# Window attention and two feed-forward layers: weights decoded in pairs, scores and values handled for two groups at once, and one fixed order for three engines

## The chip, the core and the metric

The kernel runs on one core of a Trainium2 chip. The metric is the device time of one execution in microseconds (us); less is better. TensorE (PE in the rows, PEld its weight loads) does the matrix products, VectorE (DVE), ScalarE (ACT) and GpSimd (POOL) the elementwise work, and SyncE (SP) issues every DMA of this kernel.

## What is computed

```python
# q, k, v: (4, 8, 576, 64) float32; weights arrive as float64
scores = q @ k.T / sqrt(64);  window: 0 <= pos_q - pos_k < 64, else -1e9
attn = softmax(scores);  x = (attn @ v) -> (2304, 512)
x = maximum(maximum(x @ w1, x @ w2), x @ w3) @ w_out        # 512 -> 768 -> 512
h = x @ w_in                                               # 512 -> 2048
g = h where h >= 1, 0 where h <= -1, else (h + 1)**2 / 4
out = g @ w_out2                                           # 2048 -> 512, float32 (2304, 512)
```

## The kernel before

The 2304 tokens are 36 groups of 64 queries (9 for each batch entry). The first stage works on 9 blocks of 256 tokens (4 groups each), the second on blocks of 512.

**Weights.** Each float64 weight tile (128 rows by 512 columns) is loaded by one 512 KB DMA into a staging buffer `wst` (`w_load`, 4 buffers) and decoded by `w_split` into a high and a low float32 part: two ACT passes over the two 32-bit words (L165, then L108 with `wst` as output), a DVE shift (L169) and a DVE add (L170) into `wt`, an ACT copy for the high part (`u<-wt` or `v<-wt`) and a POOL subtraction for the low part (L111). 24 tiles belong to the first feed-forward layer (buffers `u`), 32 to the second (8 in buffers `v`, then the 24 `u` again). Every product is three matmul passes: high by high, high by low, low by high.

**Attention**, for a group: `load` and `vload` bring q, k, v; `prep` transposes q and k (on PE and out of PSUM for groups 0 to 15, on DVE after that); `qk` makes 8 score matmuls into `sps` (L288) and, right behind them, four DVE reductions with the mask (L293, result `sm` and the row minimum `nm`); `ex` is four ACT exponentials; `norm` a DVE reciprocal and a POOL product; `ptr` four PE transposes into `pps` and `ptc` their ACT copy; `pv` 8 matmuls into `ops` (L342), an ACT copy and a DVE subtraction into the token tile `xt`. `sps` and `ops` are one PSUM tile each with room for two groups.

**First feed-forward layer**, for a block: 18 `a_item`s (L363, 12 matmuls each, PSUM tile `ps` out of 3 buffers), three of which make one of six hidden tiles: ACT copies the first product (`ht`), DVE takes two maxima (L372), ACT and POOL split the result into `h`. Then four `b_item`s (L385, 18 matmuls), whose result ACT copies to `x2s` (2 buffers) and SP stores to `x_scratch`.

**Order.** Everything of the first stage gets a place on a time line in units of one `a_item`; `put` collects, a sort sets the order. From the third block on, groups are handled in pairs at *visits*, one each 12 units: at a visit PE does `pv` of one pair, `ptr` of the next, `qk` of the one after. The `b_item`s of a block come `BD` = 6 items into the next block. From the first visit on, each step's PE instructions are tied behind those of the step before (`chained`, `tc.issue_after`); the scheduler sets everything else, and the whole of the start. Shortly before the last block (`put(begin[...] - 0.1, None)`, the *turn* below) the attention's memory is given to the second layer, whose weights follow by `w2_next`.

**Second layer**: for each block and hidden tile, `c_mm` (L541, 12 matmuls), `c_act` (two ACT, three DVE instructions) and, three steps later, `d_item` (L606, 12 matmuls). `x2_split` loads (`x2r`) and splits the block's input.

Of the kernel before, what the change touches and what calls it, by code (L numbers as in the profile page):

```python
# [21 lines left out]
NW = 4  # L22
# [26 lines left out]
EXP = (1.1, 2.1)  # L49
PTC = (0.6, 1.6)  # L50

# [3 lines left out]
    "T2 X2 T3 X3 W6"  # L55
# [5 lines left out]
def kernel(ctx, tc, q, k, v, w1, w2, w3, wo1, wi2, wo2, out, x2d):  # L61
# [92 lines left out]
    def w_split(key, st, eng):

        s = wslot[key]
        hi, lo = st[:, :, 1], st[:, :, 0]
        t = stg.tile([P, 512], I32, tag="wt", name="wt", bufs=WT)
        nc.scalar.activation(  # L165
            hi.bitcast(F32), hi.bitcast(F32), AF.Prelu, scale=2.0 ** (WS - 119), alpha=2.0 ** 32
        )
        act_copy(lo, lo.bitcast(U32), scale=2.0 ** -29)
        nc.vector.tensor_scalar(t, hi, 3, None, op0=ALU.logical_shift_left)  # L169
        nc.vector.tensor_tensor(t, t, lo, op=ALU.add)  # L170
        act_copy(s[:, 0:512], t.bitcast(F32))
        sub(eng, s[:, 512:1024], t.bitcast(F32), f32(s[:, 0:512]))

    def w_col(key, hl, kt):
        return wslot[key][:, hl * 512 + kt * P: hl * 512 + (kt + 1) * P]
# [14 lines left out]
    def load(g):  # L190
# [15 lines left out]
        if g not in pet and (g - PET) % CH == 0:  # L206
            for nm, src in (("q", q), ("k", k)):
                t = stg.tile([P, NP, 2 * CH, 32], F32, tag="wst", name="raw", bufs=NW)
# [12 lines left out]
                chunk[nm, (g - PET) // CH] = t  # L221

    def vload(g):
        b, i, s = blk(g)
        s0 = i * BL
        d = st_g[g]
        if g == 0:
            return
        t = apool.tile([P, H, D], F32, tag="vr", name="vr", bufs=5)
# [45 lines left out]
    def qk(g):  # L275
        d = st_g[g]
        win, mask, W = window(g)
        sm = apool.tile([P, NP, 2 * BL], F32, tag="sm", name="sm", bufs=5)
# [3 lines left out]
        for x in range(2):  # L282
            for bank in range(2):
                p = 2 * bank + x
                for h in range(2):
# [4 lines left out]
                    )  # L290

        for p in range(NP):
# [4 lines left out]
        d.update(sm=sm, nm=nm, W=W)  # L297

    def ex(g):
        d = st_g[g]  # L300
        W, sm = d["W"], d["sm"]
        ss = apool.tile([P, NP], F32, tag="ss", name="ss", bufs=5)
        for p in range(NP):
# [3 lines left out]
        d["ss"] = ss  # L307
# [19 lines left out]
    def ptc(g):  # L327
# [3 lines left out]
        act_copy(pt[0:W], d["pps"][0:W])  # L331
        d["pt"] = pt

    def pv(g, xt, off):
# [10 lines left out]
        act_copy(xt[:, 0, :, off:off + BL], ops)  # L345
        sub(nc.vector, xt[:, 1, :, off:off + BL], ops, f32(xt[:, 0, :, off:off + BL]))
# [47 lines left out]

    def x2_split(tb, pool, kt):
        t0, n = blocks2[tb]
        if kt == 0:
            x2t[tb] = pool.tile([P, 2, KD, N2], F32R, tag="x2t", name="x2t", bufs=1)
        x = x2t[tb]
        r = pool.tile([P, N2], F32, tag="x2r", name="x2r", bufs=2)  # L400
        nc.sync.dma_start(r[:, 0:n], x2d[kt, :, t0:t0 + n])
        act_copy(x[:, 0, kt, 0:n], r[:, 0:n])
        sub(nc.vector, x[:, 1, kt, 0:n], r[:, 0:n], f32(x[:, 0, kt, 0:n]))
# [26 lines left out]
    def pv_x(g):  # L430
        j, o = gblock[g]
        if o == 0:
            xt_new(j)
        pv(g, xts[j], o)
# [37 lines left out]
    for cost, fn, args in seq:  # L472
# [3 lines left out]
        if args[0] == 0:  # L476
            put(at + 0.5, w_next, nc.gpsimd)
# [7 lines left out]
    stages = (load, vload, prep, qk, ex, norm, ptr_c, pv_x)  # L485
    ops0 = dict(L=load, V=vload, P=prep, Q=qk, E=ex, N=norm, T=ptr_c, X=pv_x)
    for x, tok in enumerate(SEQ.split()):
        if tok[0] == "W":
            for _ in range(int(tok[1:] or 1)):
                put(-100 + 0.1 * x, w_next, nc.gpsimd)  # L490
# [30 lines left out]
    put(begin[len(blocks1) - 1] - 0.1, None)  # L521

    order2 = [(w, f) for f in range(KF2) for w in (4, 5)]
    slots2, w2n = [], [0]

    def w2_next():
        n = w2n[0]
        if n < len(order2):
            w, f = order2[n]
            st = w_load((w, f), wi2 if w == 4 else wo2, slots2[n], "col" if w == 4 else "row", f)  # L530
            w_split((w, f), st, nc.gpsimd)
            w2n[0] += 1
# [14 lines left out]
    tail = [None]  # L547

    def chained(fn, *args):

        if tail[0] is None:
            fn(*args)
        else:
            with tc.issue_after(tail[0]):
                fn(*args)
        pe = [i for i in nc.cur_bb.bb.instructions[-200:] if i.engine == mybir.EngineType.PE]
        if pe:
            tail[0] = pe[-1]

    for at, _, fn, args in order:  # L560
        if fn:
            if (fn, args) == (b_item, (len(blocks1) - 1, 0)):
                c_mm(0, 0, pacc, "acc")
            if at < visits[0]:
                fn(*args)
            else:
                chained(fn, *args)
        else:
# [3 lines left out]
            slots2 += [p2.tile([P, 1024], F32R, name=f"v{i}") for i in range(2 * KF2 - NU)] + U  # L572
            for kt in range(KD):
                x2_split(0, p2, kt)
            for _ in range(4):
                w2_next()
# [42 lines left out]
    for x, (tb, f) in enumerate(seq):  # L619
# [39 lines left out]
```

## Time and profile before

| | |
|---|---|
| median of 3 runs | 863.98 us (861.62 to 864.16) |
| the profiled execution's own time | 864.39 us |
| its span, first to last instruction | 862.3 us |
| PE busy / DVE / ACT / POOL | 798.3 / 363.9 / 356.2 / 157.9 us |
| mean granted clock of TensorE | 0.985 of full |

The span is what a page of the profile divides up; 2.1 us of the execution's own time lie around it. Busy times are those of single engines and overlap each other. "Idle before" in a row is the time that the engine stood still just ahead of it, with the instruction that released it.

### The profile page before, as it was taken

The page shows a single profiled execution, that of the slowest core. Times are in us where ns is not written, and L with a number is a line of the kernel's source. Part 1 is how long each engine was busy: PE and PEld are TensorE (multiplying, and loading weights), DVE is VectorE, ACT ScalarE, POOL GpSimd, SP SyncE. Part 2 cuts the span into 40 slices and gives each one's busy share as a digit, 9 for nine tenths or more (in the row PEclk, how much of TensorE's full clock was granted, in tenths as well). Part 3 has the DMA queues.
Part 4 walks back from the last instruction along what each step waited for, and adds up shares of the span by engine and source line. Part 5 has one row for each costly group of instructions (what it writes and reads, how often), then busy time and mean ns, then how long its engine had stood idle before and what let it go on. Part 6 is the DMA issues. An engine that isn't in the chain of part 4 may idle for free.

```text
span 862.3 us, 14835 instructions
## 1 busy us (share of the span) xinstructions
PE 798.3 (93%) x5776; PEld 701.6 (81%) x5776; DVE 363.9 (42%) x937; ACT 356.2 (41%) x871; POOL 157.9 (18%) x157
## 2 busy tenths in 40 slices
PE   6698889999999898999779999999999999999998
PEld 4597778889898888898778888888888888888896
DVE  5778422323333432316678733433343334333343
ACT  6988533333333534324779422322232223222232
POOL 3666311111111121213574200000000000000000
PEclk8899999999999999999989999999999999999999
DMA  9976243233141413003777000100020001000000
GB/s 243 279 216 187 43 84 85 52 70 63 40 80 32 135 26 98 14 26 111 234 222 241 24 1 25 62 0 1 1 74 0 1 1 36 25 1 1 24 26 25
DMA packets 128054, 62.70 MB, mean 73 GB/s; under 512 B 98288, under 2 KB 120816, under 8 KB 127984
## 3 DMA queue, kind: packets, MB, share of 16 engines
q1 hardware_dynamic: 127984, 61.76, 26.2%
q8 instruction: 45, 0.74, 0.4%
q14 instruction: 25, 0.20, 0.1%
HBM read 52.30 MB, written 9.44 MB: 72 GB/s over the span
## 4 chain that ended last, share of the span: by engine, by line
PE 77%; DVE 5%; DMA 4%; ACT 4%; issue 2%; SPq 1%; POOL 1%; DVEq 0%; ACTq 0%; POOLq 0%
PE acc L606 23%; PE hp L541 23%; PE ps L363 18%; PE ps L385 7%; DMA wst<-in_moe_w_in 3%; PE ops L342 2%; PE sps L288 2%; PE pps L324 1%; DVE sm L293 1%; SPq L215 1%; DVE wt L170 1%; DMA x2r<-x_scratch 1%; ACT wst L165 1%; DVE wt L169 1%; ACT wst L108 1%
## 5 line engine op out<-in xcount | busy, mean ns | idle before, releaser
L363 PE MATMUL ps<-xt,u 128*128 128x256 f32 x1944 | 239.1, 283 | 9.1 <-DVE ht L372 4.0
L363 PEld LDWEIGHTS ps<-xt,u 128*128 128x128 f32 x1944 | 232.5, 190 | 13.9 <-DVE ht L372 5.2
L541 PE MATMUL hp<-x2t,u 128*128 128x512 f32 (+1 forms) x720 | 161.6, 372 | 0.0
L606 PE MATMUL acc<-u,g 128*128 128x512 f32 x648 | 160.4, 396 | 0.0
L586 ACT ACTIVATE u<-hp,half 128x512 f32<-128x512 f32 (+1 forms) x80 | 51.5, 644 | 251.6 <-PE hp L541 251.5
L541 PEld LDWEIGHTS hp<-x2t,u 128*128 128x128 f32 x720 | 126.9, 188 | 27.2
L606 PEld LDWEIGHTS acc<-u,g 128*128 128x128 f32 x648 | 120.9, 188 | 28.3
L589 DVE SCALAR_TENSOR_TENSOR gt<-u,hp 128x512 f32<-128x512 f32 (+1 forms) x80 | 50.6, 632 | 165.8 <-ACT u L587 165.7
L372 DVE TENSOR_TENSOR ht<-ps,ht 128x256 f32<-128x256 f32 x108 | 45.4, 421 | 131.3 <-PE ps L363 114.0
L385 PE MATMUL ps<-h,u 128*128 128x256 f32 x648 | 82.8, 287 | 4.8 <-ACT h L108 2.4
L385 PEld LDWEIGHTS ps<-h,u 128*128 128x128 f32 x648 | 79.7, 194 | 7.2 <-ACT h L108 2.6
L111 POOL TENSOR_TENSOR u<-wt,u 128x512 fp32r<-128x512 f32 x48 | 67.5, 1408 | 46.7 <-ACT u L108 44.3
L111 POOL TENSOR_TENSOR h<-ht,h 128x256 fp32r<-128x256 f32 x54 | 42.7, 793 | 129.0 <-ACT h L108 128.7
L315 POOL TENSOR_TENSOR sm<-sm,rs 128x512 f32<-128x512 f32 (+1 forms) x36 | 35.8, 994 | 142.4 <-DVE rs L314 130.3
L304 ACT ACTIVATE sm<-sm,nm 128x128 f32<-128x128 f32 (+1 forms) x144 | 55.2, 388 | 15.2 <-DVE nm L293 15.2
L170 DVE CUSTOM_DVE_ANT_0 wt<-wst,wt 128x1024 uint16<-128x1024 uint16 x56 | 56.2, 1004 | 3.5 <-ACT wst L108 0.6
L108 ACT ACTIVATE h<-ht 128x256 fp32r<-128x256 f32 x54 | 22.3, 414 | 83.7 <-DVE ht L372 83.6
L606 PE MATMUL acc<-v,g 128*128 128x512 f32 x216 | 53.6, 394 | 0.0
L541 PE MATMUL hp<-x2t,v 128*128 128x512 f32 (+1 forms) x240 | 53.5, 371 | 0.0
L593 DVE CAST g<-gt 128x512 fp32r<-128x512 f32 (+1 forms) x80 | 34.2, 428 | 45.5 <-PE acc L606 43.1
L111 DVE TENSOR_TENSOR g<-gt,g 128x512 fp32r<-128x512 f32 (+1 forms) x80 | 51.1, 639 | 2.7
L541 PEld LDWEIGHTS hp<-x2t,v 128*128 128x128 f32 x240 | 41.9, 188 | 8.3
(50 smaller groups left out, 627.6 us busy)
## 6 DMA issues: line engine op xcount, KB each, us to landing
wst<-in_moe_w_out SPq DMA_DIRECT2D x22, 512.0 KB, 4.4
wst<-in_moe_w SPq DMA_DIRECT2D x18, 512.0 KB, 5.7
wst<-in_moe_w_in SPq DMA_DIRECT2D x16, 512.0 KB, 4.3
vr<-in_v SPq DMA_DIRECT2D x24, 256.0 KB, 3.0
x_scratch<-x2s SPq DMA_DIRECT2D x36, 128.0 KB, 1.8
out<-ob SPq DMA_DIRECT2D x18, 256.0 KB, 2.0
x2r<-x_scratch SPq DMA_DIRECT2D x16, 256.0 KB, 2.9
vr<-in_v SPq DMA_DIRECT2D x19, 128.0 KB, 3.4
```

The source lines that it names most:

```text
L111: eng.tensor_tensor(dst, a, b, op=ALU.subtract)
L170: nc.vector.tensor_tensor(t, t, lo, op=ALU.add)
L304: nc.scalar.activation(sm[:, p, 0:W], sm[:, p, 0:W], AF.Exp, bias=d["nm"][:, p:p + 1], scale=-1.0, accum_out=ss[:, p:p + 1])
L315: nc.gpsimd.tensor_tensor(sm[:, :, 0:W], sm[:, :, 0:W], rs.unsqueeze(2).to_broadcast([P, NP, W]), op=ALU.mult)
L363: nc.tensor.matmul(ps[:, 0:n], w_col((w, f), wl, kt), xt[:, xl, kt, 0:n], start=(x == 0), stop=(x == len(passes) - 1))
L372: nc.vector.tensor_tensor(t[:, 0:n], ps[:, 0:n], part[j, f][:, 0:n], op=ALU.max)
L385: nc.tensor.matmul(ps[:, 0:n], w_col((3, f), wl, dt), hts[j, f][:, xl, 0:n], start=(x == 0), stop=(x == len(passes) - 1))
L541: nc.tensor.matmul(ps[:, 0:n], w_col((4, f), wl, kt), x2t[tb][:, xl, kt, 0:n], start=(x == 0), stop=(x == len(passes) - 1),)
L586: nc.scalar.activation(u[:, 0:n], ps[:, 0:n], AF.Relu, bias=half, scale=2.0 ** (-WS / 2 - 1))
L589: nc.vector.scalar_tensor_tensor(gt[:, 0:n], u[:, 0:n], 2.0 ** WS, ps[:, 0:n], op0=ALU.min, op1=ALU.max)
L593: nc.vector.tensor_copy(g[:, 0, 0:n], gt[:, 0:n])
L606: nc.tensor.matmul(accs[t], g[:, gl, t * P:(t + 1) * P], wslot[5, f][:, wl * 512:(wl + 1) * 512], start=(f == 0 and x == 0), stop=(f == KF ...
```

## The change

Weights are loaded and decoded in pairs of tiles: two DMAs fill one staging buffer of twice the size (3 in place of 4), and each of the six decoding instructions works on 1024 columns. The raw q and k of a chunk share one such buffer, and the input of a block of the second layer comes in one DMA into such a buffer.

At a visit, the score matmuls of both groups come first; their reductions (`red`) and exponentials follow in halves of two head pairs between the next items. The value matmuls of both groups come first too, and one copy and one subtraction (`values`) take both. For odd groups below 8, DVE and not ACT copies the transposed weights of the attention. `sm` and `vr` have 4 buffers, not 5.

The first block's `b_item`s come after 2 items of the second block, not 6. From the first visit on, the steps are tied on PE, ACT and DVE. The second layer's weights get places in the order: the first pair one block ahead of the turn, nine more every 3.6 units from the turn on, each decoded 6 units after its load; the other six in the second layer's first block.

```diff
-NW = 4
+NW = 3
...
+RED = (0.3, 2.3)
-EXP = (1.1, 2.1)
+EXP = (1.7, 3.7)
...
+EW = 1
+W2STEP = 3.6
+W2LAG = 6
+W2IN = 10
...
-    "T2 X2 T3 X3 W6"
+    "T2 X2 T3 X3 W3"
...
+    def w_load(pair, slot):
+        st = stg.tile([P, 1024, 2], I32, tag="wst", name="wst", bufs=NW)
+        for x, (w, f) in enumerate(pair):
+            o = st[:, 512 * x:512 * x + 512]
...
-        t = stg.tile([P, 512], I32, tag="wt", name="wt", bufs=WT)
+        t = stg.tile([P, 1024], I32, tag="wt", name="wt", bufs=WT)
...
-        act_copy(s[:, 0:512], t.bitcast(F32))
-        sub(eng, s[:, 512:1024], t.bitcast(F32), f32(s[:, 0:512]))
+        act_copy(s[:, 0], t.bitcast(F32))
+        sub(nc.gpsimd, s[:, 1], t.bitcast(F32), f32(s[:, 0]))
...
+    def red(g, pairs=range(NP)):
...
+        for p in pairs:
             nc.vector.tensor_tensor_reduce(
...
-        act_copy(pt[0:W], d["pps"][0:W])
+        if g < 8 and g % 2:
+            nc.vector.tensor_copy(pt[0:W], d["pps"][0:W])
+        else:
+            act_copy(pt[0:W], d["pps"][0:W])
...
-        act_copy(xt[:, 0, :, off:off + BL], ops)
-        sub(nc.vector, xt[:, 1, :, off:off + BL], ops, f32(xt[:, 0, :, off:off + BL]))
+    def values(g, n, xt, off):
+        o = ops2[:, g % 2:g % 2 + n].rearrange("a g p c -> a p g c")
+        hl = [xt[:, x, :, off:off + n * BL].rearrange("a p (g c) -> a p g c", g=n) for x in range(2)]
+        act_copy(hl[0], o)
+        sub(nc.vector, hl[1], o, f32(hl[0]))
...
+        r = x2r[tb] = stg.tile([P, KD, N2], F32, tag="wst", name="x2r", bufs=NW)
+        nc.sync.dma_start(r[:, :, 0:n], x2d[:, :, t0:t0 + n].rearrange("k p n -> p k n"))
...
-        seq += items[:BD] + late + items[BD:]
+        bd = 2 if j == 1 else BD
+        seq += items[:bd] + late + items[bd:]
...
             put(vq + 0.02, qk, g)
-            put(vq + EXP[y], ex, g)
-            put(vq + EXP[y] + 1, norm, g)
+            for z in range(2):
+                put(vq + RED[y] + z, red, g, (2 * z, 2 * z + 1))
+                put(vq + EXP[y] + z, ex, g, (2 * z, 2 * z + 1))
+            put(vq + EXP[y] + 2, norm, g)
...
-            put(vp, pv_x, g)
+            put(vp, pv, g)
+        put(vp + 0.04, val, g1, 2)
...
+    for n in range(W2IN):
+        at = begin[len(blocks1) - 2] + 1 if n < EW else turn + 0.35 + W2STEP * (n - EW)
+        put(at, w2_load, n)
+        put(at + W2LAG, w2_split, n)
...
+    TIED = (mybir.EngineType.PE, mybir.EngineType.Activation, mybir.EngineType.DVE)
...
+            chained(fn, *args, tie=at >= visits[0])
...
         if tb == 0:
-            w2_next()
-            w2_next()
+            if W2IN + f < KF2:
+                w2_load(W2IN + f)
+            if 1 <= f <= KF2 - W2IN:
+                w2_split(W2IN + f - 1)
```

How the instructions of three places stand in the queues, before and after:

First place, PE's queue at a visit in the middle of the first stage (values of groups 10 and 11 in `ops`, transposes of 12 and 13 in `pps`, scores of 14 and 15 in `sps`). Before, with the engines whose semaphores an instruction waits on:

```order
L342 MATMUL ops_103<-pt,vr 64x64 x8
L342 MATMUL ops_103<-pt,vr 64x64 [waits DMAHW1_49,DVE_49]
L342 MATMUL ops_103<-pt,vr 64x64 x7
L324 MATMUL pps<-ident,sm 128x128 [waits Pool_49]
L324 MATMUL pps<-ident,sm 128x128 x3
L324 MATMUL pps<-ident,sm 128x128 [waits Pool_49]
L324 MATMUL pps<-ident,sm 128x128 x3
L288 MATMUL sps_102<-kring,qt_1656 64x128 x8
L288 MATMUL sps_102<-kring,qt_1656 64x128 [waits DVE_49]
L288 MATMUL sps_102<-kring,qt_1656 64x128 x7
```

The same visit after the change:

```order
L361 MATMUL ops_92<-pt,vr 64x64 x8
L361 MATMUL ops_92<-pt,vr 64x64 [waits DMAHW0_49]
L361 MATMUL ops_92<-pt,vr 64x64 x7
L340 MATMUL pps<-ident,sm 128x128 [waits Pool_49]
L340 MATMUL pps<-ident,sm 128x128 x3
L340 MATMUL pps<-ident,sm 128x128 [waits Pool_49]
L340 MATMUL pps<-ident,sm 128x128 x3
L298 MATMUL sps_91<-kring,qt_1546 64x128 x16
```

The order of the matmuls is the same; the waits on DVE ahead of the second group's values and scores are gone.

Second place, PE's queue at the start, from the transposes of group 3's attention weights to the first items. Before (`qt_430` belongs to groups 6 and 7, `u_61` is the first weight tile):

```order
L324 MATMUL pps<-ident,sm 128x128 x4
L342 MATMUL ops_103<-pt,vr 64x64 x8
L288 MATMUL sps_102<-kring,qt_430 64x128 x16
L363 MATMUL ps<-xt,u_61 128x256
L363 MATMUL ps<-xt,u_62 128x256
```

After (`qt_357` belongs to groups 4 and 5, `u_61` is the first pair of tiles):

```order
L340 MATMUL pps<-ident,sm 128x128 x4
L361 MATMUL ops_92<-pt,vr 64x64 x8
L259 MATMUL tp<-ident,nat 128x128 x4
L298 MATMUL sps_91<-kring,qt_357 64x128 x8
L259 MATMUL tp<-ident,nat 128x128 x4
L361 MATMUL ops_92<-pt,vr 64x64 x8
L298 MATMUL sps_91<-kring,qt_357 64x128 x8
L387 MATMUL ps<-xt,u_61 128x256 x2
```

The scores of groups 6 and 7 no longer stand ahead of the first item; those of groups 4 and 5 still do.

Third place, ACT's queue behind the turn, among the `b_item`s of the eighth block. Before (a decoding is L165, `wst<-wst`, `u<-wt`):

```order
L108 ACTIVATE x2s<-ps 128x256
L108 ACTIVATE v_5228<-wt 128x512
L165 ACTIVATE wst<-wst 128x512
L108 ACTIVATE wst<-wst 128x512
L108 ACTIVATE x2s<-ps 128x256
L108 ACTIVATE u_61<-wt 128x512
L165 ACTIVATE wst<-wst 128x512
L108 ACTIVATE wst<-wst 128x512
L108 ACTIVATE x2s<-ps 128x256
```

After (a decoding is L174, `wst<-wst`, `v<-wt` or `u<-wt`):

```order
L115 ACTIVATE x2s<-ps 128x256 x2
L174 ACTIVATE wst<-wst 128x1024
L115 ACTIVATE wst<-wst 128x1024
L115 ACTIVATE v_5092<-wt 128x1024
L115 ACTIVATE x2s<-ps 128x256
L115 ACTIVATE ht_5328<-ps 128x256
L174 ACTIVATE wst<-wst 128x1024
L115 ACTIVATE wst<-wst 128x1024
L115 ACTIVATE v_5093<-wt 128x1024
L115 ACTIVATE h<-ht_5365 128x256
```

The three ACT instructions of a decoding now stand together, and the evictions only between decodings; before, the last copy of one tile and the first two passes of the next stood between two evictions, so no eviction was queued behind a whole decoding.

## Rows read from the trace of the kernel before

**Rows 1.** Windows by stage: length, then busy time (instructions) of each engine, clock, DMA.

```profile
0.00:36.40 36.40, 21.32 (x244) 16.20 (x244) 23.77 (x95) 29.30 (x87) 14.92 (x23) 0.84 0.96 257
36.40:98.30 61.90, 56.71 (x536) 53.81 (x533) 44.64 (x113) 48.41 (x127) 38.65 (x33) 0.96 0.64 179
98.30:395.30 297.00, 267.74 (x2807) 255.61 (x2805) 88.05 (x386) 111.16 (x363) 52.55 (x63) 1.00 0.27 60
395.30:458.40 63.10, 52.64 (x387) 49.10 (x386) 45.87 (x63) 45.48 (x89) 37.79 (x30) 0.95 0.68 214
458.40:862.30 403.90, 399.85 (x1814) 326.86 (x1812) 161.53 (x281) 121.84 (x207) 14.03 (x9) 1.00 0.08 27
```

**Rows 2.** Waits of PE from 100 to 395 us: total, times, longest.

```profile
PE ops L342 <- DVE xt L111: 13.2, 14, 0.9
PE sps L288 <- DVE nm L293: 12.4, 12, 1.1
PE tp L249 <- ACT x2s L108: 2.2, 1, 2.2
```

**Rows 3.** Timeline, PE at one visit: start, length, engine, line.

```profile
144.77 0.69 PE L342 MATMUL ops<-pt,vr 128*64 128x64 f32 x16
...
146.40 0.69 PE L342 MATMUL ops<-pt,vr 128*64 128x64 f32 x16 [0.94 <-DVE xt L111]
...
149.76 0.67 PE L288 MATMUL sps<-kring,qt 64*64 64x128 f32 x16 [1.06 <-DVE nm L293]
...
150.36 2.37 PE L385 MATMUL ps<-h,u 128*128 128x256 f32 x18
```

**Rows 4.** Timeline of the start.

```profile
33.89 0.40 ACT L108 ACTIVATE xt<-ops 128x256 fp32r<-128x256 f32 x1
...
36.43 4.08 PE L363 MATMUL ps<-xt,u 128*128 128x256 f32 x25
...
89.55 1.27 POOL L111 TENSOR_TENSOR u<-wt,u 128x512 fp32r<-128x512 f32 x1 [0.15 <-ACT u L108]
...
98.34 2.26 PE L385 MATMUL ps<-h,u 128*128 128x256 f32 x18
```

**Rows 5.** The chain that ended last: undisturbed items and steps (start, length).

```profile
152.73 15.40 PE ps L363 x132
...
183.24 6.30 PE ps L385 x54
...
449.37 9.16 PE ps L385 x55
...
480.60 2.79 PE hp L541 x12
```

**Rows 6.** Groups by line: decoding, and one 256-column copy; busy, mean ns, idle before.

```profile
L111 POOL TENSOR_TENSOR u<-wt,u 128x512 fp32r<-128x512 f32 x48 | 67.5, 1408 | 46.7 <-ACT u L108 44.3 <-PE acc L606 1.7 <-PE ps L385 0.3
L170 DVE CUSTOM_DVE_ANT_0 wt<-wst,wt 128x1024 uint16<-128x1024 uint16 x56 | 56.2, 1004 | 3.5 <-ACT wst L108 0.6
...
L165 ACT ACTIVATE wst<-wst 128x512 f32<-128x512 f32 x56 | 37.6, 672 | 15.9 <-DMA wst<-in_moe_w_in 10.6 <-DMA wst<-in_moe_w_out 4.5 <-DMA wst<-in_moe_w 0.7
L108 ACT ACTIVATE wst<-wst 128x512 int32<-128x512 uint32 x56 | 37.5, 669 | 0.0
L169 DVE TENSOR_SCALAR wt<-wst 128x512 int32<-128x512 int32 x56 | 37.0, 661 | 19.8 <-POOL u L111 12.5 <-ACT wst L165 4.3 <-POOL v L111 1.4
...
L108 ACT ACTIVATE u<-wt 128x512 fp32r<-128x512 f32 x48 | 30.2, 629 | 10.9 <-DVE wt L170 10.4
...
L108 ACT ACTIVATE h<-ht 128x256 fp32r<-128x256 f32 x54 | 22.3, 414 | 83.7 <-DVE ht L372 83.6
```

**Rows 7.** Timeline at the turn: two DVE adds and a POOL subtraction.

```profile
421.48 0.69 DVE L170 CUSTOM_DVE_ANT_0 wt<-wst,wt 128x1024 uint16<-128x1024 uint16 x1
...
435.78 1.30 POOL L111 TENSOR_TENSOR u<-wt,u 128x512 fp32r<-128x512 f32 x1 [1.29 <-ACT u L108]
...
436.17 1.47 DVE L170 CUSTOM_DVE_ANT_0 wt<-wst,wt 128x1024 uint16<-128x1024 uint16 x1
```

More of the change, by code (lines that the diff above doesn't have):

```diff
@@ L206, in load @@
         if g not in pet and (g - PET) % CH == 0:
-            for nm, src in (("q", q), ("k", k)):
-                t = stg.tile([P, NP, 2 * CH, 32], F32, tag="wst", name="raw", bufs=NW)
+            raw = stg.tile([P, 2, NP, 2 * CH, 32], F32, tag="wst", name="raw", bufs=NW)
+            for y, (nm, src) in enumerate((("q", q), ("k", k))):
+                t = raw[:, y]
                 x = 0
@@ L290, in qk @@
                     )
-        for p in range(NP):
+        d.update(sm=sm, nm=nm, W=W)
+    def red(g, pairs=range(NP)):
+        d = st_g[g]
+        _, mask, W = window(g)
+        sm, nm = d["sm"], d["nm"]
+        for p in pairs:
             nc.vector.tensor_tensor_reduce(
@@ L296, in qk, with ex @@
             )
-        d.update(sm=sm, nm=nm, W=W)
-    def ex(g):
+    def ex(g, pairs=range(NP)):
         d = st_g[g]
         W, sm = d["W"], d["sm"]
-        ss = apool.tile([P, NP], F32, tag="ss", name="ss", bufs=5)
-        for p in range(NP):
+        if pairs[0] == 0:
+            d["ss"] = apool.tile([P, NP], F32, tag="ss", name="ss", bufs=5)
+        ss = d["ss"]
+        for p in pairs:
             nc.scalar.activation(
@@ L306, in ex @@
             )
-        d["ss"] = ss
     def norm(g):
@@ L330, in ptc, with pv @@
         pt = apool.tile([P, NP, P], F32, tag="pt", name="pt", bufs=3)
-        act_copy(pt[0:W], d["pps"][0:W])
+        if g < 8 and g % 2:
+            nc.vector.tensor_copy(pt[0:W], d["pps"][0:W])
+        else:
+            act_copy(pt[0:W], d["pps"][0:W])
         d["pt"] = pt
-    def pv(g, xt, off):
+    def pv(g):
         d = st_g[g]
@@ L428, with val @@
             gblock[(t0 + o) // BL] = (j, o)
-    def pv_x(g):
+    def val(g, n=1):
         j, o = gblock[g]
@@ L433, in pv_x, with qk_r @@
             xt_new(j)
-        pv(g, xts[j], o)
+        values(g, n, xts[j], o)
+    def pv_x(g):
+        pv(g)
+        val(g)
+    def qk_r(g):
+        qk(g)
+        red(g)
     order = []
@@ L476 @@
         if args[0] == 0:
-            put(at + 0.5, w_next, nc.gpsimd)
+            put(at + 0.5, w_next)
         at += cost
@@ L489 @@
             for _ in range(int(tok[1:] or 1)):
-                put(-100 + 0.1 * x, w_next, nc.gpsimd)
+                put(-100 + 0.1 * x, w_next)
         else:
@@ L515, with w2_load, w2_split @@
             put(vq + 0.02, qk, g)
-            put(vq + EXP[y], ex, g)
-            put(vq + EXP[y] + 1, norm, g)
+            for z in range(2):
+                put(vq + RED[y] + z, red, g, (2 * z, 2 * z + 1))
+                put(vq + EXP[y] + z, ex, g, (2 * z, 2 * z + 1))
+            put(vq + EXP[y] + 2, norm, g)
             put(vt + 0.01, ptr, g)
             put(vt + PTC[y], ptc, g)
-            put(vp, pv_x, g)
[L521 to L532, printed above, removed]
+            put(vp, pv, g)
+        put(vp + 0.04, val, g1, 2)
+    slots2, staged = list(V), {}
+    def w2_load(n):
+        staged[n] = w_load(((4, n), (5, n)), slots2[n])
+    def w2_split(n):
+        w_split(slots2[n], staged.pop(n))
+    turn = begin[len(blocks1) - 1]
+    put(turn - 0.1, None)
+    for n in range(W2IN):
+        at = begin[len(blocks1) - 2] + 1 if n < EW else turn + 0.35 + W2STEP * (n - EW)
+        put(at, w2_load, n)
+        put(at + W2LAG, w2_split, n)
     hps = {}
@@ L546, with chained @@
     order.sort(key=lambda e: e[:2])
-    tail = [None]
-    def chained(fn, *args):
-        if tail[0] is None:
-            fn(*args)
[L553 to L558, printed above, removed]
+    tails = defaultdict(list)
+    def chained(fn, *args, tie=True):
+        ends = {}
+        with ExitStack() as stack:
+            for i in [i for e in tails for i in tails[e]] if tie else ():
+                stack.enter_context(tc.issue_after(i))
+            n = len(nc.cur_bb.bb.instructions)
+            fn(*args)
+        for i in nc.cur_bb.bb.instructions[n:]:
+            if i.engine in TIED:
+                ends[i.engine] = i
+        for e, i in ends.items():
+            tails[e] = [i] if tie else tails[e] + [i]
+    TIED = (mybir.EngineType.PE, mybir.EngineType.Activation, mybir.EngineType.DVE)
     for at, _, fn, args in order:
@@ L562 @@
             if (fn, args) == (b_item, (len(blocks1) - 1, 0)):
[L563 to L567, printed above, removed]
+                chained(c_mm, 0, 0, pacc, "acc")
+            chained(fn, *args, tie=at >= visits[0])
         else:
```

65 lines of the change are left out of this document (31 added, 34 removed).

## The prediction

> **What bounds the kernel now.** I read the windows by stage first [rows 1]. From 458.4 us on PE is busy 399.85 of 403.9 us: the second layer runs at PE's own rate, and the change leaves its products alone. What can be won lies ahead of it, where PE stands idle 15.1 us to 36.4, 5.2 us to 98.3, 29.3 us to 395.3 and 10.5 us to 458.4, 60 of the 64 us in which PE does nothing.
>
> Next I read PE's waits in the third stretch [rows 2]. Fourteen times the second group's value matmuls wait 0.94 us for the DVE subtraction of the first group, twelve times the second group's score matmuls wait 1.05 us for the first group's reductions, and once the transposes wait 2.2 us behind a store that stands among the raw loads on SP. Together 27.8 of the 29.3 us. One visit shows how [rows 3]: it lasts from 144.77 to 150.36, 5.6 us, and 2.0 of these are the two waits. Nothing else happens on PE meanwhile, since its queue is in order.
>
> The start is bound by ACT, DMA and order together: DMA moves 257 GB/s, 96% of its engines busy, and ACT is busy 29.3 of 36.4 us [rows 1]. The turn (395.3 to 458.4) holds 372 first-layer matmuls and 12 of the second layer. At the undisturbed rates, 15.40 / 132 = 0.117 us and 2.79 us for 12 [rows 5], that is 43.4 + 2.8 = 46.2 us; it took 63.1, so 16.9 are lost, 10.5 as idle time and the rest in slow matmuls. The 55 that took 9.16 us would have taken 6.4, the mean clock of the stretch is 0.95 of full, so some ran at the lower of the two levels. ACT (45.5 us) and DVE (45.9 us) were busy with weights there.
>
> **The change, part by part.** The sum is made against the profiled execution's 864.4 us, 0.4 above the median.
>
> *Visits.* PE's queue after the change has the second group's values and scores with no wait on DVE behind the first group (first place shown). Both reads of `ops` and all reductions now follow PE's work, not part it, and the next visit, 12 units or about 20 us later, comes long after they are done. So 13.2 + 12.4 us go. The work itself, four reductions and four exponentials a group, stays and lies beside the next items: DVE is busy 88 and ACT 111 of 297 us there. Queued behind it now are the item evictions, and an item may wait for one; PE has three `ps` buffers, about 4 us of work, as cover, and the ACT work between a visit and the first `ht` copy is about 3.7 us. The 2.2 us behind the raw loads should go too, as the first block's stores come 4 items earlier, ahead of most of the next chunk's loads; 1.5 us of small waits remain. I take −27; the bounds are −29.3, all idle time, and −20, if a third of the gain comes back as late evictions.
>
> *Decoding.* No row shows 1024 columns. An ACT pass lies between the 0.67 of 512 columns and twice that, 1.34. A copy of 256 columns takes 0.41 and of 512 0.63 [rows 6], 0.21 for 256 more, so I take 0.42 more for 512 more: 1.09, 1.09 and 1.05, 3.2 us a pair in place of 2 × 1.97 = 3.9. DVE's shift and add (0.66 and 1.00) lie between 1.7 and 3.3 us, POOL's subtraction (1.41) between 1.4 and 2.8; I take the upper ends, as their time is nearly all columns. So ACT saves 0.7 us on each of 28 pairs and the others nothing. The four transposed copies given to DVE take about 0.6 us each off ACT, 2.4 us in all, and put as much on DVE, which has 12.6 us free before 36.4. One ACT copy of 512 columns for the values saves little and is hidden by the next item, as are the joined input loads, which come 2 steps of 5.6 us ahead of their use.
>
> *Start.* The last values that the first item needs were copied by ACT at 33.89, and the item began at 36.43 [rows 4] behind the scores of groups 6 and 7, which are no longer ahead of it (second place). Adding up what ACT now has ahead of that copy, 20 us of work from 5 us on, held up by the third pair, which lands behind 1.8 MB of q, k, v and 3.1 MB of weights (19 us at 257 GB/s, and by my estimate 4 more for issue and landing), I get 29.5 for the copy and 30.5 for the item, 6 us earlier. From there the weights set the pace. Ahead of the last pair of the first layer SP now issues 18.4 MB, 72 us at 257 GB/s; with 8 us to decode the last pair, the first `b_item` can't start before 80. I take 84. It stood at 98.34 [rows 4], behind 30 items where it is now behind 26; the four are 5.6 us, so the comparable time is 92.7, and 8 us are won. Bounds: 0, if the pair's longer way (1.1 + 1.1 + 2.0 + 1.05 + 2.8 us, against half) uses up what the order gives, and −13 at the floor.
>
> *Turn.* Before, 23 tiles were decoded in it; now six or seven pairs, one every 3.6 units or 5.0 us of PE. But ACT's three passes stand together (third place) and the last waits for DVE: 1.1 + 1.1 + 2.0 + 1.05 = 5.3 us, in which no eviction can pass, and the DVE maxima stand behind the pair's shift and add likewise. With three `ps` buffers PE covers 4.2 us. I followed the queues through the stretch: no stall in the eighth block's `b_item`s, then 2.7, 1.0 and 2.8 us at three of the four following hidden tiles, and about 2.5 in two places at the end, 9 us lost in place of 16.9. I take −8. Bounds: −14, if little more than the drains is lost, and +2, if DVE's steps are held up by POOL as below and a pair holds ACT 7 us, 1.7 more at six pairs.
>
> *Second layer.* Nine pairs are left for its first steps, where before it were eight tiles. A step gives 5.6 us of PE as cover. Without weights a step costs ACT 1.5 and DVE 2.0 us (121.8 and 161.5 us over 80 steps [rows 1]); with a pair that makes 4.7 and 5.3 us. That fits, narrowly, and the first steps have pairs in hand. I take +1; bounds 0 and +4.
>
> Sum: 864.4 − 27 − 8 − 8 + 1 = 822.4, so **822 us**. The bounds give 808 and 850.
>
> **The rivals.** *The turn keeps its loss.* A DVE add took 0.69 us with POOL idle, and 1.47 where it began 0.4 us into a POOL subtraction [rows 7], ending 0.56 after it. With both twice as long, a DVE step that meets the subtraction of the pair before waits up to 2.8 us, twice what it does now, and the whole tied decoding with it: 7 us on ACT, and 831 us (828 to 836). The Trainium skill, page "SBUF — State Buffer", section "Who interferes with whom", states it as a rule: the two engines share a port pair that the first one holds for its whole instruction; the rows agree (1.47 against 0.69). For it speaks that POOL's subtraction of one pair starts right when the next decoding may; against it, that the first 1.1 us of that is an ACT pass which needs no DVE, and most of the overlap is then over.
>
> *The start wins nothing,* since the last pair is ready no earlier: before, the last subtraction began at 89.55 [rows 4], 9 us before the first `b_item`, so weights were not all that held it. DMA fell to 179 GB/s after 36.4 [rows 1], which speaks for room. Time: 830. Both of these together: 838.
>
> *The waits at the visits come back on other engines:* reductions stand among the maxima on DVE, a late maximum holds `ps`, and half of the 25.6 us returns: 835. Against it: DVE is busy 30% there.
>
> *Slower than before.* The tied decodings part PE's work wholly: each of nine pairs stops PE for 7 us, as the evictions of all three buffers stand behind it. The stretch then takes 46 + 63 = 109 us, 46 more, and the kernel 864 + 46 − 35 = 875. It decides from 16.9 + 35 = 52 us lost, 5.8 us of standing PE a pair; against it stand the three buffers.
>
> **How the numbers follow.** My forecast 0.50, with a range of its own from 812 to 829; the turn keeps its loss 0.17; the start wins nothing 0.14; both 0.06; waits come back 0.07; slower 0.04; better than 808 0.02. Leaving out the last two, the far half of waits that come back and of both together, and some of the tails, the range for 8 in 10 is 808 to 840. A measurement of this kernel can tell about 0.3%, 2.6 us, from no change. All cases but one end well below that: faster 0.94, same 0.02, slower 0.04.
>
> **What the profile after would show.** Visits right: 14 visits of 3.6 us with no PE wait on `xt` or `nm`, and under 5 us of idle PE in the 280 us after the first `b_item`s; wrong: PE waits on `ht` or `x2s` right behind a visit. Decoding right: ACT passes of 1.0 to 1.15 us, POOL near 2.7. Start right: first item at 29 to 32, first `b_item` at 81 to 87. Turn right: 52 to 58 us from the last values to the second layer's steady run, with idle PE for evictions behind `v<-wt` or `u<-wt`; wrong: 63 or more, with DVE steps of 3 us and over beside POOL. Second layer right: 404 us. What would make the forecast wrong altogether is a start in which PE waits for pairs again and again at the lower clock, or a turn in which it stands behind each of them.

## The result, and the profile after

The changed kernel took 825.54 us (median of 4 runs, 824.94 to 828.82), the kernel before 862.8 us on the same chip (4 runs): a ratio of 0.958, 95% interval 0.954 to 0.961. The profiled execution took 825.81 us, its span is 824.0. The forecast was 822, range 808 to 840. The sum came out 3.5 us low; of its four terms two were right, one was too large by 8 us and one too small by 4. These two errors take each other off in part, so that the total is as close as it is partly by luck.

The windows by stage, columns as in [rows 1]: to the first item, to the first `b_item`, to the end of the last values, to the second layer's steady run, to the end.

```profile
0.00:34.50 34.50, 20.21 (x208) 14.92 (x208) 19.56 (x69) 25.06 (x63) 13.63 (x18) 0.79 0.96 262
34.50:92.70 58.20, 51.80 (x512) 48.77 (x513) 42.96 (x98) 44.13 (x96) 36.82 (x23) 0.95 0.72 193
92.70:367.90 275.20, 270.85 (x2862) 262.86 (x2861) 89.03 (x392) 102.61 (x354) 57.37 (x66) 0.99 0.30 69
367.90:418.80 50.90, 47.28 (x389) 46.05 (x386) 22.50 (x30) 28.93 (x44) 18.53 (x13) 1.00 0.43 144
418.80:824.00 405.20, 400.21 (x1814) 326.86 (x1812) 180.03 (x283) 136.47 (x213) 24.44 (x10) 1.00 0.11 40
```

The first `b_item` now stands behind 26 items, not 30. With the 5.6 us of these four put on the right side, before had 92.7, 302.5, 63.1 and 403.9 us [rows 1, 4]. So the start won 0, the middle 27.3, the turn 12.2, and the second layer lost 1.3: 38.2 of the span's 38.3.

PE's waits from 92 to 368 us, to be held against [rows 2]:

```profile
PE ps L387 <- ACT x2s L115: 4.0, 4, 2.9
PE ps L387 <- ACT ht L115: 0.3, 1, 0.3
```

One visit on PE, as [rows 3]:

```profile
138.53 1.15 PE L361 MATMUL ops<-pt,vr 128*64 128x64 f32 x32
139.61 1.09 PE L340 MATMUL pps<-ident,sm 128*128 128x128 f32 x8
140.63 1.10 PE L298 MATMUL sps<-kring,qt 64*64 64x128 f32 x32
141.66 2.37 PE L409 MATMUL ps<-h,u 128*128 128x256 f32 x18
```

3.1 us in place of 5.6 (3.6 was forecast), without a wait inside.

The start, PE and POOL, as [rows 4]:

```profile
34.51 5.49 PE L387 MATMUL ps<-xt,u 128*128 128x256 f32 x24 [2.70 <-ACT xt L115]
...
82.39 2.39 POOL L118 TENSOR_TENSOR u<-wt,u 128x1024 fp32r<-128x1024 f32 x1 [0.58 <-ACT u L115]
...
92.74 2.26 PE L409 MATMUL ps<-h,u 128*128 128x256 f32 x18
```

The last pair is ready at 84.8, 6 us earlier than the last tile before, and yet the first `b_item` starts 8 us behind it: PE itself was late, for the first item came at 34.5 and PE stood idle for 6.4 of the next 58.2 us. What it waited behind is a round through POOL, DVE and ACT, to be seen between 56 and 67 us (the engines apart):

```profile
56.79 2.40 POOL L118 TENSOR_TENSOR u<-wt,u 128x1024 fp32r<-128x1024 f32 x1 [2.30 <-ACT u L115]
61.44 2.39 POOL L118 TENSOR_TENSOR u<-wt,u 128x1024 fp32r<-128x1024 f32 x1 [0.58 <-ACT u L115]
```

```profile
57.14 3.13 DVE L179 CUSTOM_DVE_ANT_0 wt<-wst,wt 128x2048 uint16<-128x2048 uint16 x1
...
62.49 1.89 DVE L178 TENSOR_SCALAR wt<-wst 128x1024 int32<-128x1024 int32 x1 [1.02 <-ACT wst L174]
```

```profile
60.30 1.06 ACT L115 ACTIVATE u<-wt 128x1024 fp32r<-128x1024 f32 x1 [2.09 <-DVE wt L179]
...
66.10 1.06 ACT L115 ACTIVATE u<-wt 128x1024 fp32r<-128x1024 f32 x1 [0.82 <-DVE wt L179]
```

The add that begins 0.35 us into POOL's subtraction ends 1.08 us after it and takes 3.13 us; alone it takes 1.2. ACT's copy waits for that add, POOL's next subtraction for that copy, and again DVE has to stand by: a round of 5.1 us a pair (six copies from 55.65 to 81.26), with evictions in ACT's queue behind the waiting copy. The Trainium skill, page "SBUF — State Buffer", section "Who interferes with whom", has the shared port pair as its rule; these rows agree. That the round is what cost the time was a theory until the second experiment.

How the round reaches PE is plainest in its longest wait, 3.18 of the 6.4 us: POOL's subtraction, DVE's add beside it, ACT's copy behind the add, an `ht` copy behind that, and PE.

```profile
77.75 2.40 POOL L118 TENSOR_TENSOR u<-wt,u 128x1024 fp32r<-128x1024 f32 x1 [2.26 <-ACT u L115]
78.74 2.48 DVE L179 CUSTOM_DVE_ANT_0 wt<-wst,wt 128x2048 uint16<-128x2048 uint16 x1 [1.23 <-ACT wst L115]
81.26 1.06 ACT L115 ACTIVATE u<-wt 128x1024 fp32r<-128x1024 f32 x1 [2.25 <-DVE wt L179]
82.22 0.64 ACT L115 ACTIVATE ht<-ps 128x256 f32<-128x256 f32 x2
82.64 1.67 PE L387 MATMUL ps<-xt,u 128*128 128x256 f32 x12 [3.18 <-ACT ht L115]
```

The turn, ACT and then PE:

```profile
389.38 1.06 ACT L115 ACTIVATE v<-wt 128x1024 fp32r<-128x1024 f32 x1 [1.83 <-DVE wt L179]
390.34 0.37 ACT L115 ACTIVATE x2s<-ps 128x256 f32<-128x256 f32 x1
...
401.75 1.06 ACT L115 ACTIVATE u<-wt 128x1024 fp32r<-128x1024 f32 x1 [1.67 <-DVE wt L179]
402.71 0.37 ACT L115 ACTIVATE ht<-ps 128x256 f32<-128x256 f32 x1
```

```profile
390.76 10.33 PE L387 MATMUL ps<-xt,u 128*128 128x256 f32 x84 [1.57 <-ACT x2s L115]
403.13 4.47 PE L387 MATMUL ps<-xt,u 128*128 128x256 f32 x36 [2.04 <-ACT ht L115]
```

The stalls are of the forecast kind, an eviction behind `v<-wt` or `u<-wt`, but there are only two of them, and the clock stays at 1.00 of full (0.95 before).

### The profile page after: what moved, and what is told of

The parts are those of the page before. It is cut to its first block, busy times and chain, and to the rows that moved or that the text cites. A ratio compares the mean times of both kernels' runs of the same rounds, so it can differ in the third digit from the quotient of the medians.

```text
span 824.0 us, 14535 instructions
## 1 busy us (share of the span) xinstructions
PE 790.4 (96%) x5776; PEld 699.5 (85%) x5776; DVE 354.1 (43%) x871; ACT 337.2 (41%) x769; POOL 150.8 (18%) x129
## 4 chain that ended last, share of the span: by engine, by line
PE 75%; ACT 6%; DVE 6%; SPq 5%; DMA 4%; issue 3%; POOL 0%; DVEq 0%; ACTq 0%; POOLq 0%
PE acc L648 22%; PE ps L387 21%; PE hp L583 21%; PE ps L409 6%; SPq L225 4%; DVE wt L179 3%; DMA wst<-in_moe_w_out 2%; ACT wst L174 2%; PE ops L361 2%; DVE wt L178 2%; PE pps L340 1%; PE sps L298 1%; DMA x_scratch<-x2s 1%; ACT wst L115 1%; ACT sm L321 1%
## 5 line engine op out<-in xcount | busy, mean ns | idle before, releaser
L409 PE MATMUL ps<-h,u 128*128 128x256 f32 x648 | 79.4, 281 | 0.0
L409 PEld LDWEIGHTS ps<-h,u 128*128 128x128 f32 x648 | 77.0, 188 | 1.2 <-issue 1.0
L118 POOL TENSOR_TENSOR u<-wt,u 128x1024 fp32r<-128x1024 f32 x24 | 60.0, 2506 | 58.7 <-ACT u L115 58.7
L118 DVE TENSOR_TENSOR g<-gt,g 128x512 fp32r<-128x512 f32 (+1 forms) x80 | 59.5, 744 | 2.7
L635 DVE CAST g<-gt 128x512 fp32r<-128x512 f32 (+1 forms) x80 | 37.7, 471 | 42.5 <-PE acc L648 39.6
L648 PEld LDWEIGHTS acc<-v,g 128*128 128x128 f32 x216 | 40.3, 188 | 8.9
```

The lines of the kernel that those rows point to most:

```text
L118: eng.tensor_tensor(dst, a, b, op=ALU.subtract)
L409: nc.tensor.matmul(ps[:, 0:n], w_col((3, f), wl, dt), hts[j, f][:, xl, 0:n], start=(x == 0), stop=(x == len(passes) - 1))
L635: nc.vector.tensor_copy(g[:, 0, 0:n], gt[:, 0:n])
L648: nc.tensor.matmul(accs[t], g[:, gl, t * P:(t + 1) * P], wslot[5, f][:, wl], start=(f == 0 and x == 0), stop=(f == KF2 - 1 and x == 2),)
```

## The experiments

Stages in us from PE's timeline of each profile; the medians are of 4 runs (`e8` of 5). A row's stages add up to the span of its profiled execution, whose own time lies up to 2.9 us from the median (`e7`). The turn ends with the first step of the second layer behind the last `b_item`. Before is shown with the four items moved; so is `e1`, which has the old place of the first `b_item`s. "Lost" is the turn less the 46.2 us of its matmuls. How finely a stage can be read: PE's order in `e4` is that of the changed kernel up to the turn, and its start reads 1.3 us longer, its middle 2.5 shorter. Differences of a stage below 2.5 us are not told apart.

| kernel | median | start | middle | turn (lost) | second layer |
|---|---|---|---|---|---|
| before | 862.8 | 92.7 | 302.5 | 63.1 (16.9) | 403.9 |
| changed | 825.5 | 92.7 | 275.2 | 50.9 (4.7) | 405.2 |
| e1 visits alone | 829.8 | 90.8 | 272.3 | 59.3 (13.1) | 403.9 |
| e2 low parts on DVE | 820.0 | 86.0 | 274.4 | 50.9 (4.7) | 405.0 |
| e3 halves | 827.5 | 96.1 | 270.0 | 48.3 (2.1) | 411.5 |
| e4 a pair each 2.4 units | 840.0 | 94.0 | 272.7 | 60.7 (14.5) | 410.2 |
| e5 ties on PE alone | 846.9 | 94.6 | 281.0 | 65.1 (18.9) | 406.0 |
| e6 e2, stores by ACT | 828.8 | 86.1 | 279.3 | 52.9 (6.7) | 408.8 |
| e7 e2, fewer pairs ahead | 826.2 | 86.5 | 273.8 | 52.4 (6.2) | 408.8 |
| e8 no change at the visits | 868.2 | 98.6 | 310.4 | 52.3 (6.1) | 405.2 |
| e9 e2, halves in the turn | 817.2 | 86.0 | 276.1 | 48.3 (2.1) | 404.9 |
| e10 `pt` copies on ACT | 822.9 | 89.0 | 276.5 | 51.0 (4.8) | 405.2 |
| e11 e9 and e10 | 814.8 | 85.7 | 273.6 | 48.3 (2.1) | 405.2 |

**e1**, the kernel before with the change at the visits alone.

```diff
...
-            put(vq + EXP[y], ex, g)
...
+            for z in range(2):
+                put(vq + RED[y] + z, red, g, (2 * z, 2 * z + 1))
+                put(vq + EXP[y] + z, ex, g, (2 * z, 2 * z + 1))
...
-            put(vp, pv_x, g)
+            put(vp, pv, g)
+        put(vp + 0.04, val, g1, 2)
```

> The kernel before with the change at the visits alone (scores of both groups first, reductions and exponentials in halves, values of both groups first and read out together); loading, decoding, ties and the turn stay as before. My theory, that the order at the visits removes the two waits of 0.94 and 1.05 us at each of 14 visits and nothing else: 27 us less between the first b_items and the last values, start and turn within 2 us of before, in all 836 us (833 to 840). Rival, that the ties on ACT and DVE are what keeps the waits from coming back: half of the 27 us or less, 849 us or more, with waits of PE for evictions behind the visits.

829.8 us (ratio 0.962, 0.960 to 0.964), 6 below the expectation: the middle gave 30 us, and 4 came in the turn, with the old number of decodings. No tie on ACT or DVE is needed for the visits' gain; the rival falls. Everything else in the change together is worth 4 us: the turn wins 8 on top, and start, middle and second layer give some of it back (1.9, 2.9 and 1.3 us, about what a stage can tell).

**e2**, the changed kernel, low parts of the first layer's pairs on DVE.

```diff
-            w_split(U[n // 2], w_load(order1[n:n + 2], U[n // 2]))
+            w_split(U[n // 2], w_load(order1[n:n + 2], U[n // 2]), nc.vector)
```

> The changed kernel, with the low-part subtraction of the first layer's 12 pairs on DVE and no longer on POOL. My theory of why the start won nothing: from 56 to 85 us a pair comes every 5.1 us because POOL's subtraction (2.4 us) keeps the next pair's DVE add waiting and ACT's next copy stands behind that add; with the subtraction on DVE a pair should come every 4.1 us or so, the pace of the DMA, the first b_item at 86 instead of 92.7 and the kernel at 819 us (816 to 822). Rival, the DMA sets the pace of the pairs: first b_item at 92 to 93 and 825 us. Rival, the order in which items and pairs stand on ACT sets it: 825 us too, but with pairs that are ready earlier than they are used.

820.0 us, first `b_item` at 85.99, as expected. Its window from first item to first `b_item`:

```profile
34.20:86.00 51.80, 51.23 (x513) 48.53 (x514) 43.63 (x107) 44.34 (x96) 15.99 (x14) 0.94 0.79 215
```

PE's idle time fell from 6.4 to 0.6 us, and DMA rose from 193 to 215 GB/s, so its pace was not the limit. The last six copies of the pairs, 25.6 us apart from first to last in the changed kernel, are 18.5 us apart here (55.00 to 73.53), 3.7 us a pair. The groups by line (busy, mean ns) of both kernels tell why; changed first, then `e2`:

```profile
L179 DVE CUSTOM_DVE_ANT_0 wt<-wst,wt 128x2048 uint16<-128x2048 uint16 x28 | 40.0, 1427 | 6.1 <-ACT wst L115 4.4
...
L178 DVE TENSOR_SCALAR wt<-wst 128x1024 int32<-128x1024 int32 x28 | 29.0, 1037 | 25.7 <-ACT wst L174 22.5 <-POOL h L118 1.6 <-issue 1.5
```

```profile
L179 DVE CUSTOM_DVE_ANT_0 wt<-wst,wt 128x2048 uint16<-128x2048 uint16 x28 | 34.7, 1238 | 4.1 <-ACT wst L115 2.5
...
L118 DVE TENSOR_TENSOR u<-wt,u 128x1024 fp32r<-128x1024 f32 x12 | 15.7, 1312 | 0.4 <-ACT u L115 0.4
```

The subtraction takes 1.31 us on DVE and 2.4 on POOL, and the adds are held up hardly at all (1.24 us on average, 1.43 in the changed kernel).

**e3**, loads in pairs, each pair decoded in two halves.

```diff
...
+        for x in range(2):
+            c = slice(512 * x, 512 * x + 512)
+            hi, lo = st[:, c, 1], st[:, c, 0]
+            t = stg.tile([P, 512], I32, tag="wt", name="wt", bufs=2 * WT)
...
```

> The changed kernel, loaded in pairs as before this edit, but each pair decoded in two halves of 512 columns, twelve instructions for six. ACT has 0.7 us more per pair, POOL holds DVE for 1.4 us at a time and not 2.5, evictions can pass between the halves. My theory, that the width of the decoding instructions is worth next to nothing: 825 us within 3. Rival, the width is what won the turn: turn 5 us or more longer, 830 us or more. Rival, the width costs what the start should have won: first b_item at 88 or earlier, 820 us or less.

827.5 us, within the expectation, but it is a balance: the start 3 us longer, the middle 5 shorter (I have no reason for all of that; 2.9 us are waits for `x2s`), the turn 2.6 shorter, the second layer 6 longer, where PE waits 5.3 us for `gt` (1.1 in the changed kernel). The width is no gain in itself: it helps the second layer, and hurts the turn, where evictions have to pass.

**e4**, all nine pairs of the turn into it.

```diff
-W2STEP = 3.6
+W2STEP = 2.4
```

> The changed kernel with the second layer's pairs every 2.4 units in the turn instead of 3.6, so that all nine fall into it (now seven). My theory, that the turn became 12 us shorter because fewer weights are decoded in it: the turn then takes 55 to 60 us instead of 51, the second layer loses 1 us less, in all 829 to 834 us. Rival, the turn gained by the ties and the order and not by the number of weights: 824 to 827 us.

840.0 us, worse than expected. The turn's window, then PE's waits in it:

```profile
366.70:427.40 60.70, 51.84 (x387) 50.04 (x386) 30.96 (x35) 37.87 (x52) 25.85 (x15) 0.92 0.49 168
```

```profile
PE ps L387 <- DVE ht L396: 4.1, 2, 2.7
PE ps L387 <- ACT x2s L115: 3.0, 1, 3.0
PE ps L387 <- ACT ht L115: 1.1, 1, 1.1
```

Ten first passes of a decoding instead of seven, 9.8 us more lost: 3.3 us for each. Idle PE is 8.9 of the 14.5 us lost; the matmuls are slower too, at a granted clock of 0.92. So the turn came out just above the 55 to 60 us that I expected. What I had not expected is the second layer, 5.0 us longer although fewer pairs are left for it (7 of POOL's subtractions, 10 in the changed kernel): in its first steps PE waits 1.9 us for an `x2s` copy and 3.2 us for `g` and `gt`.

**e5**, ties on PE alone.

```diff
-    TIED = (mybir.EngineType.PE, mybir.EngineType.Activation, mybir.EngineType.DVE)
+    TIED = (mybir.EngineType.PE,)
```

> The changed kernel with the steps tied on PE alone, so that the scheduler orders ACT and DVE as it did before. My theory, that the ties on ACT and DVE bring nothing of their own, the visits' gain being in the order of PE's matmuls and the turn's in the smaller number of weights decoded there: 825.5 us within 3. Rival, the ties won the turn: turn 56 us or longer, 831 us or more. Rival, the ties hold evictions behind decodings: turn 48 us or less, 822 us or less.

846.9 us: my theory, that the ties bring nothing, is wrong, by 21 us. The turn alone has 14 of them. Its window:

```profile
375.60:440.70 65.10, 51.38 (x386) 49.41 (x385) 47.41 (x42) 44.94 (x60) 41.74 (x20) 0.92 0.66 223
```

The loss still goes with the number of decodings, as in e4, but it is the ties that set that number. Without them the scheduler pulls decodings forward: 12 of POOL's subtractions end in the turn (5 in the changed kernel), DMA moves 223 GB/s (144), and 3 are left for the second layer (10). A place on the time line that isn't tied on ACT and DVE did not hold here. The middle lost 5.8 us besides, with 7.7 us of PE's waits for `x2s`.

**e6**, `e2` with the stores of `x2s` issued by ACT.

```diff
-        nc.sync.dma_start(x2d[dt, :, t0:t0 + n], st[:, 0:n])
+        nc.scalar.dma_start(x2d[dt, :, t0:t0 + n], st[:, 0:n])
```

> The kernel with the low parts on DVE (820.0 us), with the stores of x2s issued from ACT's queue and no longer from SP's, where they stand behind the raw loads. My theory: PE's waits for x2s between the first b_items and the last values (4.1 us, the longest 2.9) are the stores' places on SP; they go, and ACT pays a few tenths of a us for each of 36 issues beside other work: 816.5 us (815 to 819). Rival, the waits are ACT's own order, an x2s copy behind other copies: 820 us or, with the cost of the issues, more.

828.8 us, a miss. PE's wait for `x2s` in the middle did go (4.1 to 0.2 us), but ACT now stands still behind its issues:

```profile
92.31 0.35 ACTq L414 DMA_DIRECT2D x_scratch<-x2s  x1
92.70 0.40 ACT L321 ACTIVATE sm<-sm,nm 128x128 f32<-128x128 f32 x1 [3.95 <-DMA raw<-in_k]
```

PE waits 4.0 us for `sm` and 2.7 for `ht` instead. The profile lays the 3.95 us to raw loads that SP issued; why a store of ACT waits for them stays open. So where the waits for `x2s` come from is shown, the stores' places on SP, but not a way to be rid of them.

**e7**, `e2` with 8 pairs ahead of the second layer, one each 4.4 units.

```diff
-W2STEP = 3.6
+W2STEP = 4.4
...
-W2IN = 10
+W2IN = 8
```

> The kernel with the low parts on DVE (820.0 us), with 8 of the second layer's pairs ahead of the second layer, one every 4.4 units, instead of 10 at 3.6; the other 8 are decoded in its first block. My theory, that decodings cost time in the turn and next to none in the second layer: the turn takes 48 to 50 us instead of 50.8, the second layer 405 to 407, in all 819 us (817 to 821). Rival, the second layer's first steps can't take two pairs more: second layer 410 us or more, 824 us or more.

826.2 us: the rival's time, though the second layer took 408.8 us and not 410 or more. The turn won nothing (3.0 us of its loss is one `ht` copy behind a decoding), and the second layer took 3.8 us more. But e6, with its pairs placed as in e2, has the same 408.8 us, so these 3.8 us are not shown to be the price of two pairs. With five to seven pairs the turn's loss no longer follows their number.

**e8**, the changed kernel with the old order at the visits (`qk_r` and `pv_x` for each group, `ex` whole and at its old places).

> The changed kernel with the old order at the visits (each group's reductions right behind its scores, its value copies right behind its values), all else as changed, the ties on ACT and DVE too. My theory, that the visits' gain is the order's own: 27 us or a little more come back between the first b_items and the last values, 853 us (850 to 857), with PE's waits for xt and nm of about 1 us each at 14 and 12 visits. Rival, a part of the gain belongs to the ties or the pairs: 845 us or less.

868.2 us, 0.5% slower than before (ratio 1.005, 1.003 to 1.007), and 15 more than I expected. The middle lost 35 us: PE waited 26.0 us in 25 waits of about 1 us as before and 6.7 us at one visit, where the changed kernel has 4.3 us of waits, and its matmuls took 7.0 us more, in part at a lower clock (0.98, 0.99 in the changed kernel); the start lost 5.9 to a wait for `nm`. ACT, PE and SP at the visit:

```profile
158.81 0.38 ACT L115 ACTIVATE x2s<-ps 128x256 f32<-128x256 f32 x1 [7.81 <-DMA x_scratch<-x2s]
159.09 0.38 ACT L115 ACTIVATE xt<-ops 128x256 fp32r<-128x256 f32 x1
```

```profile
159.98 1.12 PE L361 MATMUL ops<-pt,vr 128*64 128x64 f32 x16 [6.69 <-DVE xt L118]
```

```profile
148.32 8.30 SPq L225 DMA_DIRECT2D raw<-in_k  x17
156.72 0.37 SPq L414 DMA_DIRECT2D x_scratch<-x2s  x1
```

The store of an `x2s` buffer stands on SP behind 17 small loads; the next `x2s` copy waits for it on ACT; tied behind that copy is the `xt` copy that PE needs for its next eight matmuls. With the ties, a late store reaches PE through ACT; that the new order keeps a cover of some items in between is how I read the queues. So no part of the change is worth a fixed sum: that at the visits gives 33 us without ties and pairs (e1) and 43 with both.

**e9**, `e2` with the turn's pairs in halves, the second layer's at full width: 

> The kernel with the low parts on DVE (820.0 us), with the ten pairs of the turn decoded in two halves of 512 columns each and the second layer's six at full width. My theory, from the stages of the run with halves everywhere (turn 2.7 us shorter, second layer 6.3 us longer, start 3.3 longer): evictions pass between the halves, the turn takes 48 to 49 us, start and second layer stay, 818 us (815 to 820). Rival, the pairs that are left over for the second layer's first steps, decoded in halves too, cost there what the turn gains: 820 to 824 us.

817.2 us; turn 48.3, the other stages as in `e2`, as expected.

**e10**, the changed kernel without the copies on DVE.

```diff
-        if g < 8 and g % 2:
+        if False:
```

> The changed kernel with all copies of the transposed attention weights on ACT again, none on DVE. My theory, that the start is paced by the round of POOL's subtraction, DVE's add and ACT's copy from 56 us on, and that 0.6 us more on ACT for each of four groups costs nothing: 825.5 us within 3. Rival, those copies are part of what sets the first item: first item at 36 us or later, 828 us or more.

822.9 us (820.1 to 826.8; ratio to before 0.955, 0.951 to 0.959): no loss, rather a gain of 2 to 3 us that the runs' spread leaves unsettled. First item at 33.4, first `b_item` at 89.0: the copies given to DVE did not help the start.

**e11**, `e9` and `e10` together: 

> The kernel of the last run but one (low parts on DVE, the turn's pairs in halves, 817.2 us), with all copies of the transposed attention weights on ACT. If those copies on DVE delay the first item (it came at 33.4 instead of 34.5 without them, and the first b_item at 89.0 instead of 92.7), DVE, which now does the low parts too, gains by it: first b_item at 85, 816 us (814 to 817). Rival, with the low parts on DVE PE runs through from the first item to the first b_item anyway, and ACT has 2.4 us more: 817 to 819 us.

814.8 us (813.8 to 816.5), ratio to before 0.945 (0.942 to 0.948): the best version, 11 us below the changed kernel. The gain over `e9`, 2.4 us, is of the expected size, but where it came from isn't shown: the first `b_item` came at 85.7, 0.3 earlier, and the rest is below what a stage can tell. What the new place of the first `b_item`s is worth by itself wasn't tried.

## Why the prediction was right, and where it was not

*Visits, −27:* measured −27.3 in the change, −30 alone. Both waits are gone, PE is idle 4.3 us in 275 (under 5 was forecast), and e8 brings both back. Idle time fell by 24.9 us; the other 2.4 are matmuls, a term that I did not have (for one, 32 value matmuls take 1.15 us in one run, and took 0.69 us in each run of 16 before). They make up for the 2.2 us behind the raw loads, which did not go: PE still waits 4.0 us for `x2s`, and these waits are stores behind loads on SP (e6).

*Decoding:* ACT's passes took 1.15, 1.14 and 1.06 us (1.09, 1.09 and 1.05 taken), POOL's subtraction 2.51 on average (2.8). DVE's shift and add took 1.9 us undisturbed, near the 2.0 of the sums for start and turn and not at the upper end, 3.3, that I said I took. The widths were right, what they meet was not.

*Start, −8:* measured 0, the failed term. The step that failed is "from there the weights set the pace". The last pair was ready at 84.8, about when I wanted it, but PE was not: the first item came at 34.5 and not 30.5, and evictions stood behind copies that waited for DVE behind POOL. It is the time of the rival "the start wins nothing" without its reason (the last pair was not late), and the mechanism of the other rival, the shared port, in another place than I had put it. The miss of 8.7 us is the 4 us of the late item and 4.7 us more from there to the first `b_item` (58.2 where 53.5 were forecast, 6.4 of them idle PE); e2 wins 6.7 us back. Part of the late item is the pair itself: ACT stood 1.7 us until both tiles of the first had landed, with group 0's `xt` copy behind, and PE waited 3.9 us until group 0's values were read out:

```profile
13.91 1.13 ACT L174 ACTIVATE wst<-wst 128x1024 f32<-128x1024 f32 x1 [1.73 <-DMA wst<-in_moe_w]
...
17.51 0.36 ACT L115 ACTIVATE xt<-ops 128x256 fp32r<-128x256 f32 x1
```

```profile
18.38 1.12 PE L361 MATMUL ops<-pt,vr 128*64 128x64 f32 x16 [3.86 <-DVE xt L118]
```

Another part is ACT's order. PE was through with the last values that the first item needs at 31.2, but two passes of a decoding and exponentials of a later group stood ahead of their copy, and PE waited 2.7 us for it:

```profile
30.86 1.15 ACT L174 ACTIVATE wst<-wst 128x1024 f32<-128x1024 f32 x1
...
32.30 1.13 ACT L115 ACTIVATE wst<-wst 128x1024 int32<-128x1024 uint32 x1
...
34.10 0.36 ACT L115 ACTIVATE xt<-ops 128x256 fp32r<-128x256 f32 x1
```

*Turn, −8:* the mechanism was right, the size small: −12.2. I had counted 9 us of stalls; 3.6 came, and without long waits the clock stayed at full. The reason was the one given, six or seven pairs in place of 23 tiles; that the ties hold the others back was not in my working (e5). Of the rival that the turn keeps its loss little came: DVE's shift was held up by POOL's subtraction of the pair before, 1.42 us at most where it takes 0.69 alone, and the add behind it took 1.23 as alone. The ACT pass that comes first had let most of the subtraction go by, as the prediction held against the rival:

```profile
385.02 2.42 POOL L118 TENSOR_TENSOR v<-wt,v 128x1024 fp32r<-128x1024 f32 x1 [5.24 <-ACT v L115]
386.56 1.42 DVE L178 TENSOR_SCALAR wt<-wst 128x1024 int32<-128x1024 int32 x1 [2.72 <-ACT wst L174]
388.12 1.23 DVE L179 CUSTOM_DVE_ANT_0 wt<-wst,wt 128x2048 uint16<-128x2048 uint16 x1
```

*Second layer, +1:* +1.3, one wait for `gt` of 1.1 us.

*Slower than before* needed 5.8 us of standing PE a pair. Counted by first passes of a decoding beyond seven, the turn lost 3.3 us for each in e4 and 3.6 in e5; counted by POOL's subtractions beyond five, 3.3 and 2.0. So the price of a pair is only roughly known, and it shows at a density that the change keeps away from.

## What to carry to other kernels

Put work that an in-order engine does for another stage on a time line, and tie it on every engine that does it, or a scheduler may pull it to the front, where evictions stand behind it (14 us here). Where a chain goes round DVE, ACT and POOL, look at what POOL's instruction does to DVE's next: giving DVE the subtraction made a busier engine and a faster start. And before a term "the weights set the pace" is written down, add up what PE has to do from its first item on: 51 us here, which from an item at 34.2 us leads to 85, later than the floor of 80 that DMA gave.

## What the runs showed of the hardware that I had not expected

A 128x1024 subtraction took 2.4 us on POOL and 1.2 on DVE undisturbed (1.31 on average in e2), and DVE's add ran 1.21 to 1.24 us undisturbed and up to 3.13 beside POOL. Where PE waited longer its matmuls took longer too: in the turn of e4 and e5 the granted clock was 0.92, and of 14.5 and 18.9 us lost 8.9 and 13.7 were idle PE, the rest longer matmuls; in the changed kernel's turn, with 3.6 us of waits and a clock of 1.00, that rest was 1.1 us.
